# State products computed batch by batch in the layer's own layout, without a DRAM buffer, and the state tokens' weights split from resident tiles

## The chip, the cores and the metric

The kernel runs on one core of a Trainium2 chip. The metric is device time in microseconds (us), the lower the better. A core has five engines that run side by side and wait for each other through semaphores: PE (matrix products), ACT (ScalarE), DVE (VectorE), POOL (GpSimd) and SP, which here issues nearly all DMAs. PE reads its operands from SBUF (on-chip memory of 128 partitions) and writes into eight PSUM banks, from which ACT and DVE move results back to SBUF.

## The reference

Eight batches of cross attention between 512 tokens `x` and 32 state tokens, eight heads of 64, then two gated layers over all 544 tokens of a batch:

```python
a     = softmax(x @ state.T / 8);  xread = a @ state      # 512 rows a batch
a2    = softmax(state @ x.T / 8);  sread = a2 @ x         # 32 rows a batch
t     = concatenate([xread, sread])                       # heads side by side: 512 columns
h     = ((t @ w1) * (t @ w2)) @ w3 @ w_out                # first layer, d_ff 1024
out   = ((h @ w_a) * (h @ w_b)) @ moe2_w_out              # second layer, d_ff 1536
```

`x` and `state` are float32; the weights come as float64, two 32-bit words a number, and are turned into float32 on the chip. The products keep float32 accuracy: a number is split into a high and a low fp32r part (`split`), and three passes (high by high, high by low, low by high) replace one product.

## The kernel before

`w3 @ w_out` is multiplied out once (the weight products `wp`, kept as `ws`). For the x tokens, `xread @ w1` is never formed from `xread`: since `xread = a @ state`, the kernel computes the **state products** `P = state @ [w1 | w2]` per head and then multiplies by the attention weights `a`. A chunk (batch b, quarter q) of P holds, in 128 partitions (4 head pairs p of 32 state rows), two head rows r of 256 columns of w1 and 256 of w2. The layer uses it for two column blocks f (f // 2 is q).

How the state products come about. `state_product(p, nh, bg, i)` (L308) multiplies the transposed states of four batches (bg 0 or 1: 64 rows by 128 columns of `st_s`, the tile stT) with 512 columns of the converted tile `wk{p}_{nh}`: one call is two matmuls, r = 0 and 1, in the two halves of the array's rows, into two banks; as plain fp32 each is issued as two instructions. There are 4 p, 2 nh, 2 bg, 2 i: 32 calls. The result has four batches of one head pair below each other, while the layer wants one batch with its four pairs. So `product_move` (L323) copies a bank to a tile `sg` on ACT or DVE, `product_store` (L331) writes it to DRAM `p_d` in four pieces on SP's queue, `load_p` (L587) reads a chunk back, and `split_p` (L593) makes the high part on ACT and the low part on POOL.

Stages. First comes a **job stage**: jobs with guessed times are put in order by a planner (`run_jobs`, L643), which fixes each engine's order of instructions. The names in `EARLY` are loaded in that order: `wo` (rows of w_out), `w3`, `wk` (w1 and w2 by row block p and half nh) and the first three batches of x. ACT, DVE and POOL convert each; a `w3` block is then transposed by PE, split, and multiplied in a weight product of 24 matmuls. The stage also holds the attention of batches 0 and 1, the state products, and the whole first layer of batch 0 (`f`, then `x2f`). The products of bg 1 are its last filling, after the `f` jobs. Loads keep nine of the 47 SBUF units (4 KB a partition, `NUNITS`) free.

Then comes the **layer stage**: for b = 1 to 7 and f = 0 to 7, `step` (L1065) issues the product `ap` (6 matmuls), its copy on ACT, the filling `middle`, the product `bp` (6 matmuls), the product of both on DVE, the split of `h` (high on ACT, low on DVE), the filling `behind`, and at last `flush`, which accumulates the h of the step before into `x2p` (12 matmuls, four banks held for a batch). The fillings are written out by hand: the attention of the next batch in `MIDDLE` and `BEHIND`, `split_p` and `load_p` in `behind` at even f, and an `Intake` called `ab`, which converts the weights of the second layer when planned loads of the engines allow, 9 to 10 units being free. The state tokens' own rows (`one_s`, 256 columns) are interleaved with b = 7; their weights come from a second `Intake`, `sw`, which loads w1 and w2 once more by columns, converts and splits them. The second layer follows, with PE as its only busy engine.

Of the kernel before, what the change touches and what calls it, by code (L numbers as in the profile page):

```python
# [24 lines left out]
    "wo1 wo3 wo0 w3_1 wo2 w3_2 w3_0 wk0_0 x0 wk1_0 wk2_0 w3_3 "  # L25
    "w3_5 w3_6 x1 wk1_1 w3_4 wk3_0 wk0_1 x2 w3_7 wk3_1 wk2_1"
# [5 lines left out]
KEEP_SG = 2  # L32
KEEP_UNTIL = 40
STORE_BEHIND = 18

LATE_KEEP = 6
LATE_PRIO = 10
# [9 lines left out]
SW_TASKS = 2  # L47
SW_FROM = 46
# [5 lines left out]
P_AHEAD = 3  # L54
# [5 lines left out]
def attention_moe_moe2(  # L60
# [17 lines left out]
    nc = tc.nc  # L78
# [122 lines left out]
    p_d = [dp.tile([2, NP, NS, 2 * DFF1], F32, name=f"p_d{b}") for b in range(B)]  # L201
# [104 lines left out]
    sg = {}  # L306

    def state_product(p, nh, bg, i):  # L308

        for r in range(2):  # L310
            if i == 0:
                sg[p, nh, bg, r] = unit(f"sg{p}_{nh}_{bg}_{r}")
            t = pb[p, nh, bg, i, r] = bank(f"pb{p}_{nh}_{bg}_{i}_{r}")
            rows = slice(r * D, (r + 1) * D)
            nc.tensor.matmul(  # L315
                t,
                lhsT=st_s[rows, (bg * NP + p) * P : (bg * NP + p + 1) * P],
                rhs=conv[f"wk{p}_{nh}"].out[rows, half[i]],
                start=True,
                stop=True,  # L320
            )

    def product_move(p, nh, bg, i, r, eng):  # L323
        dst = sg[p, nh, bg, r].rearrange("p (q w c) -> p q w c", q=2, w=2)[:, :, i, :]
        src = flat(pb.pop((p, nh, bg, i, r)), 256)
        if eng == "A":
            nc.scalar.copy(dst, src)
        else:
            nc.vector.tensor_copy(dst, src)

    def product_store(p, nh, bg, r):  # L331
        for j in range(4):
            nc.sync.dma_start(
                out=p_d[4 * bg + j][r, p, :, nh * 1024 : (nh + 1) * 1024],
                in_=sg[p, nh, bg, r][j * NS : (j + 1) * NS],
            )
# [247 lines left out]
    p_raw = {}  # L584
    p_s = {}

    def load_p(b, q):  # L587
        t = unit(f"pr{b}_{q}")
        src = p_d[b].rearrange("r p n e -> (p n) r e")
        nc.sync.dma_start(out=flat(t, 512), in_=src[:, :, q * 512 : (q + 1) * 512])  # L590
        p_raw[b, q] = t

    def split_p(b, q):  # L593
        hi, lo = unit(f"ph{b}_{q}", F32R), unit(f"pl{b}_{q}", F32R)
        split(hi, lo, p_raw.pop((b, q)), nc.gpsimd)
        free(f"pr{b}_{q}", at=charge(A=1.1, G=2.4))
        p_s[b, q] = [t.rearrange("p (g w c) -> p g w c", g=2, w=2) for t in (hi, lo)]


# [123 lines left out]
    stores = {0: [], 1: []}  # L723

    def early_wk(p, nh):
        adds = convert_jobs(f"wk{p}_{nh}")
        last = []
        for bg in range(1):
            moves = {0: [], 1: []}
            for i in range(2):  # L730
                pr = Job(
                    "P",
                    1.0,
                    lambda a=(p, nh, bg, i): state_product(*a),
                    after=[adds[i], state_moved[bg]] + last[-1:],
                    need=2 - 2 * i,
                    keep=KEEP_SG,
                    prio=2 + len(loads) / 100,
                    banks=("ps", 2),
                )  # L740
                last.append(pr)
                for r in range(2):
                    moves[r].append(
                        Job(
                            "AV",
                            (0.6, 0.85),
                            lambda e, a=(p, nh, bg, i, r): product_move(*a, e),
                            after=[pr],
                            prio=0,
                        ).gives("ps", 1)  # L750
                    )
            for r in range(2):
                st = Job(
                    "D",
                    1.5,
                    lambda a=(p, nh, bg, r): product_store(*a),
                    after=moves[r],
                    prio=len(loads) + STORE_BEHIND,
                    lag=2.0,
                ).frees(f"sg{p}_{nh}_{bg}_{r}")  # L760
                if bg == 0:
                    stores[nh].append(st)
        return last

# [44 lines left out]

    wo_done = []  # L810
    products = []
    w_done = []
    for name in EARLY:
        if name[:2] == "wk":
            p, nh = int(name[2]), int(name[4])
            early_wk(p, nh)
# [226 lines left out]
    sw = Intake("sw", (w1, w2), None, list(range(NF1)))  # L1043
# [269 lines left out]
    last = None  # L1313
    for b, qs in ((0, range(4)), (1, range(3))):
        for q in qs:
            l = Job(
                "D",
                1.5,
                lambda b=b, q=q: load_p(b, q),
                after=stores[q // 2] + ([last] if last else []),  # L1320
                need=1,
                prio=1 + 20 * b,
                lag=1.0,
            )
            if b == 0 or q == 0:
                sp = Job("A", 1.1, lambda b=b, q=q: split_p(b, q), after=[l], need=2, prio=0 + 5 * b)
                ready[b, q] = last = Job("G", 2.4, nothing, after=[sp], prio=0 + 5 * b)
    lows = []
    mults = []
    for f in range(NF1):  # L1330
        pa = Job(
            "P",
            1.4,
            lambda f=f: first_product(f, 0),
            after=[ready[0, f // 2], attended[0][0]],
            banks=("ps", 1),
        )
# [9 lines left out]
    last = attended[0][0]  # L1347
    for p in range(NP):
        for nh in range(2):
            products = []  # L1350
            moves = {0: [], 1: []}
            for i in range(2):
                last = Job(
                    "P",
                    1.0,
                    lambda a=(p, nh, 1, i): state_product(*a),
                    after=[last],
                    need=2 - 2 * i,
                    keep=LATE_KEEP,
                    prio=LATE_PRIO,  # L1360
                    banks=("ps", 2),
                )
                products.append(last)
                for r in range(2):
                    moves[r].append(
                        Job(
                            "A", 0.6, lambda a=(p, nh, 1, i, r): product_move(*a, "A"), after=[last], prio=4
                        ).gives("ps", 1)
                    )
            frees_after(products, f"wk{p}_{nh}")  # L1370
            for r in range(2):
                Job(
                    "D",
                    1.7,
                    lambda a=(p, nh, 1, r): product_store(*a),
                    after=moves[r],
                    prio=len(loads) + STORE_BEHIND,
                    lag=2.0,
                ).frees(f"sg{p}_{nh}_1_{r}")
# [19 lines left out]
    chunks = [(b, q) for b in range(B) for q in range(4)]  # L1399

    for b in range(B):
# [9 lines left out]
        def fills1(f, b=b):  # L1411
            def middle():
                attend(MIDDLE, b, f)
                sw.run(HORIZON[0])
                ab.run(HORIZON[0])

            def behind():
                if f % 2 == 0:
                    c = 4 * b + f // 2
                    if c + 1 < len(chunks):  # L1420
                        split_p(*chunks[c + 1])
                    if c + P_AHEAD < len(chunks):
                        load_p(*chunks[c + P_AHEAD])
                        charge(D=1.5)
                else:
                    free(f"ph{b}_{f // 2}", f"pl{b}_{f // 2}")
                attend(BEHIND, b, f)
                if f == X_SLOT and b + 2 < B:
# [4 lines left out]
                if b == B - 2 and f == NF1 - 1:  # L1433
                    free("stT")
# [3 lines left out]
                if NF1 * b + f >= SW_FROM:  # L1438
                    sw.start(SW_TASKS, reserve=1)
                if NF1 * b + f >= AB_AT.get(ab.order[min(ab.next, NF2 - 1)], NF1 * B):  # L1440
                    ab.start(2, reserve=AB_RESERVE)
                sw.run(HORIZON[0])
# [13 lines left out]
    def pairs_s(f, i):  # L1456
        return [
            ([sw.cols[f][m][:, i, k, :] for m in range(2)], [sr_parts[q][:, k, :] for q in range(2)])
# [3 lines left out]
    def fills_s(f):  # L1462
        def middle():
            sw.run(HORIZON[1])
            ab.run(HORIZON[1])
            if f > 0:
                xf[0].run(1, keep=8 if sw.next < NF1 else 4)

        def behind():
            free(f"sw{f}h", f"sw{f}l")  # L1470
            sw.start(SW_TASKS, reserve=1)
            if sw.next == NF1 and f >= NF1 - 3:
# [310 lines left out]
```

## Time and profile before

| what | value |
|---|---|
| median of 3 runs | 1341.95 us (1341.14 to 1342.07) |
| profiled execution, its own time | 1342.51 us |
| its span, first to last instruction | 1340.7 us |
| PE busy in the span | 1300.3 us (97%) |
| DVE, ACT, POOL busy | 612.0, 550.2, 439.3 us |
| job stage (to the first `ap` of batch 1) | about 183 us |
| layer stage, batches 1 to 7 and the state tokens | about 183 to 560 us |
| second layer | about 560 to 1340.7 us |

The profile shows one execution. An engine's busy time is the union of its instructions; a matmul row of 0.39 us overlaps the next, which starts 0.22 to 0.23 us later. What "idle before" names is the event that ended the wait of that instruction.

### The profile page before, as it was taken

What the parts mean: (1) busy time and instruction counts of PE and PEld (TensorE: products, weight loads), DVE (VectorE), ACT (ScalarE), POOL (GpSimd) and SP (SyncE); (2) the same over time, 40 slices, a digit from 0 to 9 for tenths busy, and PEclk for the clock granted to TensorE, in tenths of its full rate; (3) what the DMA queues carried; (4) which work ended last, traced back from release to release, by engine and by line L of the source; (5) the groups of instructions that cost most, each with busy time, mean ns of one, the idle gap of its engine ahead of it and who ended that gap; (6) DMA issues with size and microseconds to landing.
All of it is one profiled execution on the core that took longest, in us unless ns stands there. A gap on an engine that the chain in (4) does not pass through costs nothing.

```text
span 1340.7 us, 17395 instructions
## 1 busy us (share of the span) xinstructions
PE 1300.3 (97%) x6596; PEld 1054.2 (79%) x6596; DVE 612.0 (46%) x792; ACT 550.2 (41%) x951; POOL 439.3 (33%) x352
## 2 busy tenths in 40 slices
PE   3998999999999999999999999999999999999998
PEld 1765768778777789888888888888888888888876
DVE  6676215646666667455532712232722326323240
ACT  7676455655565666354421412211422114221130
POOL 5554214454464477255510430110411103211100
PEclk6999999999999999999999999999999999999999
DMA  9977368493566552777373265542664434744301
GB/s 312 285 234 236 110 205 246 140 290 126 205 205 219 173 174 74 241 269 264 126 267 110 95 215 193 173 149 72 222 218 158 150 115 149 246 173 157 110 0 64
DMA packets 120662, 240.24 MB, mean 179 GB/s; under 512 B 44673, under 2 KB 65153, under 8 KB 120577
## 3 DMA queue, kind: packets, MB, share of 16 engines
q1 hardware_dynamic: 116000, 222.86, 50.5%
q0 software_dynamic: 4576, 16.26, 3.1%
q8 instruction: 52, 0.85, 0.2%
q14 instruction: 34, 0.27, 0.1%
HBM read 173.54 MB, written 65.54 MB: 178 GB/s over the span
## 4 chain that ended last, share of the span: by engine, by line
PE 89%; DMA 4%; DVE 3%; ACT 2%; issue 1%; POOL 1%; SPq 1%; ACTq 0%; POOLq 0%; DVEq 0%
PE r L1497 20%; PE o L1509 19%; PE v L1497 10%; PE x2p L1110 9%; PE bp L1051 5%; PE q L1497 5%; PE ap L1051 5%; PE abs L1552 3%; PE wp L358 2%; PE pb L315 2%; PE x2f L1291 2%; PE f L1051 1%; PE os L1581 1%; PE xt L388 1%; PE bs L1051 1%
## 5 line engine op out<-in xcount | busy, mean ns | idle before, releaser
L1509 PE MATMUL o<-z,h 128*128 128x512 f32 x1152 | 276.6, 389 | 1.3 <-ACT h L136 1.3
L1509 PEld LDWEIGHTS o<-z,h 128*128 128x128 f32 x1152 | 216.1, 188 | 47.0 <-ACT h L136 1.7
L1672 POOL TENSOR_TENSOR hb<-e,e 128x512 f32<-128x512 f32 x48 | 62.9, 1311 | 453.5 <-DVE e L1522 453.4
L136 ACT CAST h<-e 128x512 fp32r<-128x512 f32 x48 | 29.8, 621 | 364.8 <-DVE e L1675 350.8
L1110 PE MATMUL x2p<-hp,ws 128*128 128x512 f32 x672 | 161.9, 390 | 0.0
L1110 PEld LDWEIGHTS x2p<-hp,ws 128*128 128x128 f32 x672 | 125.8, 188 | 26.2
L142 POOL TENSOR_TENSOR pl<-pr,ph 128x512 fp32r<-128x512 f32 x64 | 83.1, 1320 | 120.6 <-ACT ph L136 74.0
L1522 DVE TENSOR_TENSOR e<-e,q 128x512 f32<-128x512 f32 x48 | 33.0, 688 | 195.7 <-PE q L1497 195.7
L1075 DVE TENSOR_TENSOR hfp<-asbp,bp 128x512 f32<-128x512 f32 x56 | 38.3, 684 | 93.6 <-PE bp L1051 89.9
L142 DVE TENSOR_TENSOR hp<-hfp,hp 128x512 fp32r<-128x512 f32 x56 | 54.1, 965 | 40.0 <-ACT hp L136 38.7
L1522 DVE TENSOR_TENSOR e<-e,v 128x512 f32<-128x512 f32 x48 | 33.0, 688 | 85.4 <-PE v L1497 85.4
L1497 PE MATMUL r<-xT2h,w 128*128 128x512 f32 x192 | 67.1, 390 | 0.0
L1497 PE MATMUL r<-xB11h,w 128*128 128x512 f32 x192 | 66.9, 389 | 0.0
L1497 PE MATMUL v<-xT1h,w 128*128 128x512 f32 x192 | 66.9, 389 | 0.0
L1497 PE MATMUL q<-xB21h,w 128*128 128x512 f32 x192 | 66.9, 389 | 0.0
L1497 PE MATMUL r<-xT3h,w 128*128 128x512 f32 x192 | 66.9, 389 | 0.0
L1497 PE MATMUL v<-xB22h,w 128*128 128x512 f32 x192 | 66.9, 389 | 0.0
L1497 PE MATMUL r<-xT4h,w 128*128 128x512 f32 x192 | 66.9, 389 | 0.0
L136 ACT CAST hp<-hfp 128x512 fp32r<-128x512 f32 x56 | 34.7, 620 | 57.0 <-DVE hfp L1075 52.2
L1069 ACT COPY asbp<-ap 128x512 f32<-128x512 f32 x56 | 33.1, 591 | 56.3 <-PE ap L1051 56.2
L142 DVE TENSOR_TENSOR h<-e,h 128x512 fp32r<-128x512 f32 x48 | 35.5, 739 | 33.4 <-ACT h L136 33.4
L1051 PE MATMUL bp<-ah,ph 128*128 128x512 f32 x112 | 47.9, 428 | 1.4 <-DVE a L473 0.9
(476 smaller groups left out, 2815.4 us busy)
## 6 DMA issues: line engine op xcount, KB each, us to landing
w<-w_d SPq DMA_DIRECT2D x168, 512.0 KB, 5.1
w_d<-w SPq DMA_DIRECT2D x48, 512.0 KB, 2.9
p_d<-sg SPq DMA_DIRECT2D x128, 128.0 KB, 2.5
pr<-p_d SPq DMA_DIRECT2D x32, 512.0 KB, 5.2
x<-in_x_dram SPq DMA_DIRECT2D x64, 128.0 KB, 4.6
sw<-in_moe_w_dram SPq DMA_DIRECT2D x16, 512.0 KB, 5.2
xB<-x_d SPq DMA_DIRECT2D x16, 512.0 KB, 4.8
x_d<-x2sp POOLq DMA_DIRECT2D x14, 512.0 KB, 5.8
```

Of the source, the lines that this page charges most:

```text
L136: nc.scalar.copy(hi, src)
L142: (eng or nc.vector).tensor_tensor(out=lo[:, i], in0=src[:, i], in1=hi[:, i].bitcast(F32), op=ALU.subtract)
L315: nc.tensor.matmul(t, lhsT=st_s[rows, (bg * NP + p) * P : (bg * NP + p + 1) * P], rhs=conv[f"wk{p}_{nh}"].out[rows, half[i]], start=True, ...
L1051: nc.tensor.matmul(dst[:, :n], lhsT=l[m], rhs=r[q], start=i == 0 and j == 0, stop=i == k - 1 and j == 2,)
L1069: nc.scalar.copy(a_sb[:, :n], pa[:, :n])
L1075: nc.vector.tensor_tensor(out=hf[:, :n], in0=a_sb[:, :n], in1=pb[:, :n], op=ALU.mult)
L1110: nc.tensor.matmul(acc[j], lhsT=w_s[f][:, m, j * P : (j + 1) * P], rhs=h[:, q, :n], start=per == 1 and f == 0 and i == 0, stop=f == NF1 - ...
L1497: nc.tensor.matmul(t, lhsT=w[m], rhs=xf[g].parts[x][q][:, k, :], start=first and k == 0 and i == 0, stop=k == 1 and i == 2, skip_group_che ...
L1509: nc.tensor.matmul(t, lhsT=h[:, m, part * P : (part + 1) * P], rhs=z_t[f][:, q, :], start=first and c == 0, stop=last and c == 2,)
L1522: nc.vector.tensor_tensor(out=out, in0=x, in1=y, op=ALU.add)
L1552: nc.tensor.matmul(t[:, w * 256 : (w + 1) * 256], lhsT=l[m], rhs=x_s[k][q], start=k == 0 and i == 0, stop=k == 3 and i == 2,)
L1672: nc.gpsimd.tensor_tensor(out=h2[-1][:, f % 2, :], in0=e2, in1=e5, op=ALU.mult)
```

## The change

`p_d`, `sg`, `product_move`, `product_store`, `load_p`, `split_p` and the intake `sw` go. A call `state_product(b, q)` now makes one chunk: 4 pairs p by 2 rows r, eight matmuls of 64 rows by 32 columns of `st_s` with 512 columns (two runs of 256) of `wk{p}_{q // 2}`; pair p goes to partitions 32p and up, r to the one or the other of two banks. `product_high` takes the high part from a bank on ACT, `product_low` the low part on DVE, straight from PSUM. There are again 32 calls: five in the job stage (batch 0 and the first chunk of batch 1), 27 in the layer stage, in `behind`, after the attention's filling and ahead of the `flush`, by the table `STEPS_P` (f = 0, 2, 3 and 4 of a batch; 0, 2, 3, 4, 5 in batch 6; 0 and 1 in batch 7). The eight `wk` tiles and stT stay in SBUF until batch 7. There `split_weights(nh)` splits four of them at f = 0 and four at f = 2, the low parts in turn on DVE and POOL, and the state tokens' step reads these. `EARLY` has a new order.

```diff
 EARLY = (
-    "wo1 wo3 wo0 w3_1 wo2 w3_2 w3_0 wk0_0 x0 wk1_0 wk2_0 w3_3 "
-    "w3_5 w3_6 x1 wk1_1 w3_4 wk3_0 wk0_1 x2 w3_7 wk3_1 wk2_1"
+    "wo0 wo1 wo2 w3_0 wo3 w3_1 x0 w3_2 wk0_0 w3_3 wk1_0 w3_4 wk2_0 "
+    "w3_5 wk3_0 w3_6 wk0_1 w3_7 wk1_1 x1 wk2_1 wk3_1 x2"
 ).split()
...
+STEPS_P = {0: [1], 2: [2], 3: [3], 4: [4]}
+STEPS_P_LAST = ({**STEPS_P, 5: [5]}, {0: [2], 1: [3]})
...
+    def state_product(b, q):
+
+        c = b // 4 * 512 + b % 4 * NS
         for r in range(2):
...
+            pb[b, q, r] = bank(f"pb{b}_{q}_{r}")
+        for p in range(NP):
+            for r in range(2):
+                rows = slice(r * D, (r + 1) * D)
+                w = conv[f"wk{p}_{q // 2}"].out[rows].rearrange("p (w q c) -> p w q c", w=2, q=2)
+                nc.tensor.matmul(
+                    flat(pb[b, q, r], 256)[NS * p : NS * (p + 1)],
+                    lhsT=st_s[rows, c + p * P : c + p * P + NS],
+                    rhs=w[:, :, q % 2, :],
+                    start=True,
+                    stop=True,
+                )
...
+    def product_high(b, q, r):
+        if r == 0:
+            parts = unit(f"ph{b}_{q}", F32R), unit(f"pl{b}_{q}", F32R)
+            p_s[b, q] = [t.rearrange("p (g w c) -> p g w c", g=2, w=2) for t in parts]
+        nc.scalar.copy(p_s[b, q][0][:, r], flat(pb[b, q, r], 256))
+
+    def product_low(b, q, r):
+        hi, lo = (t[:, r] for t in p_s[b, q])
+        nc.vector.tensor_tensor(
+            out=lo, in0=flat(pb.pop((b, q, r)), 256), in1=hi.bitcast(F32), op=ALU.subtract
+        )
...
+    def split_weights(nh):
+        for k in range(4):
+            hi, lo = unit(f"wkh{k}_{nh}", F32R), unit(f"wkl{k}_{nh}", F32R)
+            split(hi, lo, conv[f"wk{k}_{nh}"].out, ENGINES["VG"[k % 2]])
...
             def behind():
-                if f % 2 == 0:
-                    c = 4 * b + f // 2
-                    if c + 1 < len(chunks):
-                        split_p(*chunks[c + 1])
-                    if c + P_AHEAD < len(chunks):
-                        load_p(*chunks[c + P_AHEAD])
-                        charge(D=1.5)
-                else:
+                if f % 2:
                     free(f"ph{b}_{f // 2}", f"pl{b}_{f // 2}")
                 attend(BEHIND, b, f)
+                for q in slots.get(f, []):
+                    if 4 * b + q < 4 * B:
+                        now[0] += 1.2
+                        state_product(*divmod(4 * b + q, 4))
+                        until[0] = charge(A=1.2, V=1.4)
+                        for r in range(2):
+                            product_high(*divmod(4 * b + q, 4), r)
+                            product_low(*divmod(4 * b + q, 4), r)
+                        until[0] = None
+                if b == B - 1 and f in (0, 2):
+                    split_weights(f // 2)
```

## Rows read from the trace of the kernel before

**Rows 1.** The page's head and its first part: busy us (share) xinstructions, TensorE rows.

```profile
span 1340.7 us, 17395 instructions
PE 1300.3 (97%) x6596; PEld 1054.2 (79%) x6596; DVE 612.0 (46%) x792; ACT 550.2 (41%) x951; POOL 439.3 (33%) x352
```

**Rows 2.** By stage: window, length, busy PE, PEld, DVE, ACT, POOL, clock, DMA share, GB/s.

```profile
33.00:183.00 150.00, 143.43 (x723) 99.17 (x721) 76.24 (x101) 94.09 (x178) 56.19 (x44) 0.98 0.68 209
183.00:433.00 250.00, 246.50 (x1480) 196.23 (x1479) 151.82 (x190) 142.90 (x252) 121.23 (x100) 1.00 0.66 210
433.00:540.00 107.00, 106.82 (x681) 89.67 (x680) 68.07 (x78) 69.54 (x115) 71.02 (x52) 1.00 0.43 145
540.00:760.00 220.00, 219.77 (x1157) 189.54 (x1156) 99.13 (x146) 83.88 (x145) 75.06 (x62) 1.00 0.57 204
```

**Rows 3.** Waits of PE, 40 to 185 us: total us, times, longest.

```profile
PE w3t L344 <- POOL w L182: 2.4, 2, 2.0
PE f L1051 <- ACT ph L136: 2.3, 2, 1.8
PE f L1051 <- POOL pl L142: 1.6, 3, 0.7
```

**Rows 4.** The same windows view as rows 2, for 120 to 140 us.

```profile
120.00:140.00 20.00, 17.55 (x75) 13.87 (x74) 13.07 (x16) 12.70 (x24) 10.18 (x8) 0.91 0.42 136
```

**Rows 5.** Waits of PE, 185 to 560 us.

```profile
PE xt L388 <- issue: 1.4, 1, 1.4
PE bp L1051 <- DVE a L473: 0.9, 1, 0.9
```

**Rows 6.** PE in order of time: start, us, instruction; state products alone and in a row.

```profile
140.22 0.39 PE L1051 MATMUL f<-ah,pl 128*128 128x512 f32 x1
140.54 1.13 PE L315 MATMUL pb<-wk,stT 64*128 64x512 f32 x4
...
141.94 0.39 PE L1051 MATMUL f<-al,ph 128*128 128x512 f32 x1
...
173.35 9.71 PE L315 MATMUL pb<-wk,stT 64*128 64x512 f32 x44
182.99 0.50 PE L1051 MATMUL ap<-ah,ph 128*128 128x512 f32 x1
```

**Rows 7.** The chain that ended last, in order of time: one weight product.

```profile
60.98 5.68 PE wp L358 x24
```

**Rows 8.** Groups by line: xcount, busy us, mean ns of one, idle before and its releasers.

```profile
L315 PE MATMUL pb<-wk,stT 64*128 64x512 f32 x128 | 33.7, 615 | 0.3 <-ACT sg L327 0.3
L327 ACT COPY sg<-pb 128x512 f32<-128x512 f32 x53 | 27.8, 646 | 3.5 <-PE pb L315 3.5
L136 ACT CAST ph<-pr 128x1024 fp32r<-128x1024 f32 x32 | 33.5, 1048 | 5.0 <-DMA pr<-p_d 5.0
L142 POOL TENSOR_TENSOR pl<-pr,ph 128x512 fp32r<-128x512 f32 x64 | 83.1, 1320 | 120.6 <-ACT ph L136 74.0 <-DMA p_d<-sg 17.1 <-issue 14.5
L142 DVE TENSOR_TENSOR hp<-hfp,hp 128x512 fp32r<-128x512 f32 x56 | 54.1, 965 | 40.0 <-ACT hp L136 38.7 <-DMA x<-in_x_dram 1.4
L300 DVE TENSOR_TENSOR w3l<-w3t,w3h 128x512 fp32r<-128x512 f32 x16 | 10.8, 683 | 3.8 <-ACT w3h L294 3.7
L420 DVE TENSOR_REDUCE mx<-s 128x2 f32<-128x1024 f32 x8 | 9.7, 1210 | 0.0
```

**Rows 9.** PE in order of time: one call of `scores` between two products of the layer; the next batch's call.

```profile
186.98 0.39 PE L1051 MATMUL ap<-ah,pl 128*128 128x512 f32 x1
187.30 1.09 PE L404 MATMUL st<-xt,stT 64*32 64x512 f32 x16
...
188.66 0.39 PE L1051 MATMUL bp<-al,ph 128*128 128x512 f32 x1
...
236.66 1.09 PE L404 MATMUL st<-xt,stT 64*32 64x512 f32 x16
```

**Rows 10.** PE in order of time: the first call of `scores`.

```profile
55.48 2.36 PE L404 MATMUL st<-xt,stT 64*32 64x512 f32 x16
```

More of the change, by code (lines that the diff above doesn't have):

```diff
@@ L305, in attention_moe_moe2 @@
     pb = {}
-    sg = {}
-    def state_product(p, nh, bg, i):
+    def state_product(b, q):
+        c = b // 4 * 512 + b % 4 * NS
         for r in range(2):
[L311 to L327, printed above, removed]
-        else:
[L329 to L336, printed above, removed]
+            pb[b, q, r] = bank(f"pb{b}_{q}_{r}")
[10 more added lines that the diff above has]
+                )
+    p_s = {}
+    def product_high(b, q, r):
[8 more added lines that the diff above has]
+        )
     w3_b = {}
@@ L581, in attend @@
                 until[0] = None
[L584 to L597, printed above, removed]
     class Job:
@@ L721, in split_jobs @@
         return lows
[L723 to L763, printed above, removed]
     def frees_after(after, *names):
@@ L1312, in attention_moe_moe2 @@
     ready = {}
-    last = None
-    for b, qs in ((0, range(4)), (1, range(3))):
+    for b, qs in ((0, range(4)), (1, range(1))):
         for q in qs:
[L1316 to L1321, printed above, removed]
+            pr = Job(
+                "P",
+                1.2,
+                lambda b=b, q=q: state_product(b, q),
+                after=[*wk_done[q // 2], *state_moved.values()],
                 prio=1 + 20 * b,
-                lag=1.0,
+                banks=("ps", 2),
             )
-            if b == 0 or q == 0:
-                sp = Job("A", 1.1, lambda b=b, q=q: split_p(b, q), after=[l], need=2, prio=0 + 5 * b)
-                ready[b, q] = last = Job("G", 2.4, nothing, after=[sp], prio=0 + 5 * b)
+            ready[b, q] = []
+            for r in range(2):
+                h = Job(
+                    "A",
+                    0.65,
+                    lambda b=b, q=q, r=r: product_high(b, q, r),
+                    after=[pr] + ready[b, q],
+                    need=2 - 2 * r,
+                    prio=5 * b,
+                )
+                ready[b, q].append(
+                    Job("V", 0.75, lambda b=b, q=q, r=r: product_low(b, q, r), after=[h], prio=5 * b).gives("ps", 1)
+                )
     lows = []
@@ L1344, in attention_moe_moe2 @@
         lows.append(lo)
[L1347 to L1379, printed above, removed]
     moves = []
@@ L1463, in middle @@
         def middle():
-            sw.run(HORIZON[1])
             ab.run(HORIZON[1])
             if f > 0:
-                xf[0].run(1, keep=8 if sw.next < NF1 else 4)
+                xf[0].run(1, keep=4)
         def behind():
-            free(f"sw{f}h", f"sw{f}l")
-            sw.start(SW_TASKS, reserve=1)
-            if sw.next == NF1 and f >= NF1 - 3:
+            if f % 4 == 3:
+                free(*(f"wk{q}{k}_{f // 4}" for k in range(4) for q in "hl"))
+            if f >= NF1 - 3:
                 ab.start(1, reserve=5)
-            sw.run(HORIZON[1])
             ab.run(HORIZON[1])
-            xf[0].run(1, keep=8 if sw.next < NF1 else 4)
+            xf[0].run(1, keep=4)
             if f >= NF1 - 3 and (0, 0) not in w_t and room(5):
```

37 lines of the change are left out of this document (15 added, 22 removed).

## The prediction

> **What bounds the kernel.** The page's first part comes first: PE is busy for 1300.3 of 1340.7 us [rows 1]. Whatever the change takes from ACT, DVE, POOL and the DMA queues is worth only what it takes from PE's own work or from PE's 40 us of idle time, so the next views tell where these lie. By stage [rows 2], PE idles 6.6 us of the 150 from 33 to 183 us (150 - 143.43), 3.5 of the 250 up to 433, and 0.2 in each of the next two windows, where the state tokens and the second layer begin. The rest of the 40 lies before 33 us and at the end of the second layer. The changed order of loads still has three `wo`, a `w3`, the last `wo` and a `w3` in front, so I keep the start as it is; the end is not touched. The waits of PE say what the 6.6 us are: 2.4 for POOL's conversion of a `w3` block, 3.9 for the high and low parts of a chunk of the state products, at the `f` products [rows 3]. These 3.9 are the round trip through DRAM and POOL. In the same stretch the granted clock averages 0.91 for 20 us [rows 4]; around 129 us matmuls follow each other at half speed after those waits. I put the loss at no more than 20 x 0.09 = 1.8 us, 1.2 after leaving out the part in which PE was idle anyway. In the layer stage the waits are single events of 0.9 and 1.4 us [rows 5].
>
> **PE's own work.** The matmuls of the layer, of the weight products and of the state tokens stay as they are, in number and shape. Only the 32 calls of the state product change, and the trace has both shapes. The old one alone: the second `f` after it starts 1.72 us after the last `f` before it [rows 6]; two steps of 0.23 (5.68 less 0.39, by 23 [rows 7]) belong to the products themselves, which leaves 1.26 us. In a row, 44 instructions or 11 calls take 182.99 - 173.35 = 9.64 us, 0.88 a call [rows 6]. So a group costs 0.88 a call and 0.38 for going over to it and back. The 32 calls stand in 14 groups in order of time: 28.2 + 5.3 = 33.5 us, close to the 33.7 us of the line [rows 8]. The new shape, 64 rows by 32 columns, sixteen instructions, is that of `scores`: 188.66 - 186.98 - 0.46 = 1.22 us, alone between products of the layer [rows 9]. So the eight small tiles run side by side as well as the two wide ones. But 27 of the new calls stand alone, between `bp` and `x2p`: 27 x 1.22 = 32.9 us; the five in the job stage, in three groups, cost 5 x 0.88 + 3 x 0.38 = 5.5. That is 38.4 against 33.5: **+4.9 us**. Bounds: 0 if going over were free, +6.8 if all 32 cost the old single price of 1.26.
>
> On the 0.38 us, the Trainium skill (TensorEngine Tiling (Array Packing), Key Properties) says that a change of the tiling mode drains the array, and gives no price. That rule speaks against this change, which makes some 30 groups of 14; if the drain were free the forecast would be 5 us lower.
>
> **The job stage.** Eleven of its sixteen early calls, and all sixteen late ones, leave it; that work is in the sum above. What matters is its idle time. The 3.9 us of waits for chunks go: a chunk now needs its product (about 1), a cast on ACT (0.65, as the copy to `sg`) and a subtraction on DVE (0.68, as `w3l`, which also reads PSUM) [rows 8], against copy, store, load, a cast of 1.05 and two POOL passes of 1.32. With them goes the dip of the clock, 1.2. The 2.4 us at POOL's conversions can go, because 64 POOL passes leave, or grow, because PE has less to do in between. A `w3` block feeds PE for about 5.5 us of weight product [rows 7] and one of transposes; the new order brings one `w3` in every two names, and the eleven calls that used to fill such holes (eleven at 0.88 to 1.26, 10 to 14 us) are gone or moved. Bounds of the idle time left: 0 and 6.6 + 6.5 (half of these calls uncovered). ACT is busy 94 of the 150 us [rows 2] and loses some of its copies, so I stay near the lower end and leave 2.5 us. Gain: 6.6 + 1.2 - 2.5 = **-5.3 us**.
>
> **The layer stage.** Each call adds two casts on ACT and two subtractions on DVE, 64 x 0.65 = 42 and 64 x 0.68 = 44 us in all. ACT gives back more (27.8 + 33.5 us [rows 8]), POOL gives back 83.1 and gets only eight passes for the state tokens, SP loses 128 stores and 32 loads and with them every wait on them. DVE is the engine that pays: 151.8 busy of 250 us [rows 2] is 61%; with eight passes, 5.5 us, more in a batch of 236.66 - 187.30 = 49.4 us [rows 9] it comes to some two thirds of the then 54 us. That hides the sum, not each instruction: in `behind` at f = 2 and 3 the subtractions queue behind reductions and transposes of 1.21 us each [rows 8], with the next step's product of `ap` and `bp` behind them, and until they are done two PSUM banks are held beside the four of `x2p`, the one of `read` and the two of `ap` and `bp`. PE comes to the next `bp` about 2.7 (flush) + 1.4 (`ap`) + 1 us after the call, and the chain high, low, behind a transpose takes about 5: just covered. Bounds: -3.5 (even the present waits go, since POOL is quieter) and +9.8 (one wait like the 1.4 us of [rows 5] in each of seven batches). I take **+1 us**, nearer to a stage that now waits 3.5 us in 250.
>
> **State tokens.** `sw` goes: 16 loads of half a MB, conversion and splits, all hidden today (0.2 us idle in 433 to 540 [rows 2]), so nothing is gained. `split_weights` puts four casts of 1.05 us in a row on ACT, twice, ahead of the copy of the next `ap`; PE has a flush and two products (5.4 us) before it needs that copy's bank again. **+0.5 us**, between 0 and 2 x 1.5. The resident tiles cost units: at f = 1 I count 32 of 47 held, at f = 6 some 35, so `ab` often waits for its predecessor. I cost that at nothing: six blocks have seven batches of time, and a late one costs only if the second layer, idle 0.2 us in 220, has to wait.
>
> **Sum.** +4.9 - 5.3 + 1 + 0.5 = +1.1 on the span of 1340.7: 1341.8, with 1.8 us around it 1343.6. The profiled execution was 0.56 us above the median of the runs, so against the median the forecast is **1343.0 us**. A measurement of this kernel can tell about 0.2%, 2.7 us, from no change: within 1339.3 to 1344.6 it is "the same".
>
> **The rivals.**
> *Cover everywhere (faster).* All 7.8 us of the job stage and the 3.5 of the layer stage go: 1341.95 + 4.9 - 7.8 - 3.5 = 1335.6. For it: the DVE pass on `hp` averages 0.965 us where its neighbour `w3l` of the same size takes 0.683 [rows 8], so something slows DVE that may be the 64 POOL passes. The Trainium skill (SBUF — State Buffer, Who interferes with whom) says that a DVE instruction with two SBUF inputs and a GpSimd instruction reading SBUF lock each other out; by it `hp` is slowed by POOL, and `product_low`, with one input in PSUM, is not. Against it: 27 more DVE pairs in the queue. Chance 0.31.
> *Starved job stage (slower).* The fillers are missing before the chunks are ready: the 7.8 us are not gained and half of the moved calls leave holes, 6.5. 1341.95 + 4.9 + 6.5 + 1.5 = 1355; it decides once a `w3` block takes longer to be loaded and converted than the 6.5 us that PE lives on it. Partly so, 1347. Chance 0.18.
> *DVE and banks in the layer stage (slower).* A third of a microsecond at each of 27 calls: +9 in place of the +1, 1351. For it: the queue at f = 2 and 3; against it: DVE's load. Chance 0.13.
> *The tiles don't run side by side.* The first `scores` took 2.36 us [rows 10]. At that price 32 calls cost 32 x 1.14 more, 1379. That call probably waited for the second half of its operand; the one in the layer took 1.09. Chance 0.03.
> About even has 0.35. So faster 0.31, same 0.35, slower 0.34. The range takes in the full gain and most of the slower cases: 1334 to 1354; the likeliest case alone is 1339 to 1345.
>
> **What would show it.** PE's waits for `ph` and `pl` at the `f` products are gone, the clock in that stage is 1.0, and the first `ap` comes at about 183 - (33.5 - 5.5) - 5.3, some 150 us. A group of sixteen instructions of the new product between `bp` and `x2p` costs 1.2 us, and a batch 49.4 + 4 x 1.22 = 54.3 us. No waits of `bp`, `ap` or `x2p` on DVE's low parts; PE's idle time in the layer stage under 6 us. Wrong would be: `w3t` or `wp` waiting for conversions for more than 5 us in all, `bp` or the product waiting for banks, or an `ab` block that comes late in the second layer.

## The result

The changed kernel takes **1357.99 us** (median of 4 runs, 1357.88 to 1358.09) against 1342.01 us of the kernel before in the same session: a ratio of 1.0117, 95% interval 1.0100 to 1.0135. It is slower by 16 us, outside the forecast range of 1334 to 1354.

The page of the changed kernel, against [rows 1]:

```profile
span 1356.0 us, 17687 instructions
PE 1310.8 (97%) x6980; PEld 1050.2 (77%) x6980; DVE 617.4 (46%) x829; ACT 507.0 (37%) x898; POOL 336.0 (25%) x272
```

POOL gave back 103 us and ACT 43 us, and the time became longer: as the prediction has it at its start, what the other engines give back is worth only what PE gains by it. PE is busy 10.5 us longer and idle 4.8 us longer.

The stages are best cut at three instructions of PE: the first weight product `wp`, the first `ap` of batch 1, the first `r` of the second layer. In the kernel before these stand at 32.70, 182.99 and 561.10 us. After, the windows view (columns as in [rows 2]) cut at the same three:

```profile
0.00:28.90 28.90, 9.31 (x35) 5.38 (x35) 16.96 (x22) 21.50 (x38) 16.23 (x17) 0.65 1.01 288
28.90:152.84 123.94, 114.68 (x675) 90.46 (x674) 79.88 (x106) 74.00 (x141) 48.20 (x35) 0.96 0.47 158
152.84:567.29 414.45, 411.48 (x2735) 308.97 (x2733) 235.86 (x319) 199.18 (x370) 101.78 (x85) 1.00 0.30 102
567.29:760.00 192.71, 184.74 (x940) 157.50 (x939) 75.52 (x119) 68.58 (x118) 66.94 (x54) 0.98 0.59 211
760.00:1356.00 596.00, 590.61 (x2603) 487.89 (x2601) 209.16 (x267) 143.73 (x233) 102.81 (x83) 1.00 0.43 147
```

| stretch | before | after | difference | forecast |
|---|---|---|---|---|
| to the first `ap` | 182.99 | 152.84 | -30.15 | -33.3 |
| layer and state tokens | 378.11 | 414.45 | +36.34 | +34.4 |
| second layer | 779.60 | 788.71 | **+9.1** | 0 |
| span | 1340.7 | 1356.0 | +15.3 | +1.1 |

The forecasts are the prediction's terms by stretch: -28.0 and -5.3; 27 x 1.22, +1 and +0.5; nothing. The sum is 14.2 us off: 9.1 in a stage in which the change edits nothing, 3.2 ahead of the first `ap`, 1.9 in the layer stage.

PE's waits of after, from the first `wp` to the first `ap`, then from 567 us to the end (total, times, longest):

```profile
PE w3t L338 <- POOL w L177: 6.0, 4, 2.3
PE wp L352 <- DVE w3l L294: 2.9, 1, 2.9
...
PE r L1416 <- ACT e L1556: 6.0, 1, 6.0
PE r L1416 <- DVE e L1441: 1.7, 1, 1.7
PE o L1428 <- ACT h L131: 1.3, 1, 1.3
```

The `f` products wait for the state chunks no more, so the DRAM round trip of [rows 3] is gone as forecast; conversions of `w3` wait in its place. In the second layer the last line stood before too; the two `r` lines are new. What PE waits for at 687 us, in order of time on all engines:

```profile
681.00 1.41 POOL L894 TENSOR_TENSOR ab8s<-ab 128x256 f32<-128x256 f32 x2
...
684.97 1.04 ACT L131 CAST w<-ab8s 128x1024 fp32r<-128x1024 f32 x1 [2.85 <-POOL ab8s L894]
...
686.22 0.62 ACT L131 CAST z<-ab8t 128x512 fp32r<-128x512 f32 x1 [0.20 <-POOL ab8t L177]
686.74 0.58 ACT L1556 COPY e<-r 128x512 f32<-128x512 f32 x1
687.37 0.80 PE L1416 MATMUL r<-xT2h,w 128*128 128x512 f32 x1 [5.96 <-ACT e L1556]
```

ACT was not busy: it stood at `ab8`'s cast for 2.85 us until POOL had made the sums, and the copy `e` that frees PE's bank was queued behind. It is the conversion of the last block of the second layer's weights (an `ab` block), made inside the second layer. After the wait PE runs at about half rate for a while (matmul starts 0.4 to 0.6 us apart up to 690 us, in place of 0.22 to 0.23); the granted clock of the 20 us around it is 0.83:

```profile
680.00:700.00 20.00, 14.04 (x59) 11.48 (x59) 7.21 (x9) 4.62 (x8) 7.40 (x7) 0.83 0.70 249
```

Over the whole second layer PE is idle 6.3 us longer than in the kernel before and, with the same 3542 matmuls, busy 2.8 us longer; together these are the 9.1 us.

### The profile page after: what moved, and what is told of

Same layout as the page of the kernel before. It is cut to its first block, busy times and chain, and to the rows that moved or that the text cites. A ratio compares the mean times of both kernels' runs of the same rounds, so it can differ in the third digit from the quotient of the medians.

```text
span 1356.0 us, 17687 instructions
## 1 busy us (share of the span) xinstructions
PE 1310.8 (97%) x6980; PEld 1050.2 (77%) x6980; DVE 617.4 (46%) x829; ACT 507.0 (37%) x898; POOL 336.0 (25%) x272
## 4 chain that ended last, share of the span: by engine, by line
PE 88%; ACT 5%; DVE 4%; issue 1%; POOL 1%; DMA 1%; SPq 0%; POOLq 0%; DVEq 0%; ACTq 0%
PE o L1428 19%; PE r L1416 19%; PE x2p L1045 10%; PE v L1416 9%; PE bp L986 5%; PE ap L986 5%; PE q L1416 5%; PE pb L310 2%; PE wp L352 2%; PE abs L1471 2%; PE x2f L1226 2%; PE f L986 2%; PE os L1500 1%; PE bs L986 1%; PE as L986 1%
## 5 line engine op out<-in xcount | busy, mean ns | idle before, releaser
L1045 PE MATMUL x2p<-hp,ws 128*128 128x512 f32 x672 | 165.7, 395 | 0.0
L137 DVE TENSOR_TENSOR hp<-hfp,hp 128x512 fp32r<-128x512 f32 x56 | 44.5, 795 | 40.1 <-ACT hp L131 40.1
L177 POOL TENSOR_TENSOR ab<-ab,ab 128x512 int32<-128x512 int32 x24 | 31.5, 1332 | 74.0 <-ACT asbp L1004 33.3
L137 POOL TENSOR_TENSOR al<-a,ah 128x512 fp32r<-128x512 f32 x16 | 22.8, 1444 | 107.1 <-ACT ah L131 102.2
```

The source lines that it names most:

```text
L137: (eng or nc.vector).tensor_tensor(out=lo[:, i], in0=src[:, i], in1=hi[:, i].bitcast(F32), op=ALU.subtract)
L177: nc.gpsimd.tensor_tensor(out=out, in0=out, in1=d.bitcast(I32), op=ALU.add)
L1045: nc.tensor.matmul(acc[j], lhsT=w_s[f][:, m, j * P : (j + 1) * P], rhs=h[:, q, :n], start=per == 1 and f == 0 and i == 0, stop=f == NF1 - ...
```

## The experiments

### Why the second layer lost 9 us

*The old intake of the state tokens' weights* (e1_sw). The resident `wk` tiles are no longer split and are given back in batches 6 and 7; `sw` loads, converts and splits w1 and w2 by columns as before, and the conversion of the second layer's tokens keeps eight units off, as before, until `sw` is through. The main lines:

```diff
-                if b == B - 1 and f in (0, 2):
-                    split_weights(f // 2)
...
+                if NF1 * b + f >= 46:
+                    sw.start(2, reserve=1)
```

> The changed kernel with the old intake of the state tokens' weights: sixteen loads and splits of `sw` in the shape of before from step 46 on, no resident split tiles, and the raw wk tiles given back at batch 6 and at the first steps of batch 7. The products, their places and the job stage stay as changed. Theory 1 (the 9.1 us that the second layer gained come from units: the resident tiles hold what the intake of `ab` needs, and its late blocks are forced while PE waits): the second layer goes back to some 780 us, its waits of 6.0 and 1.7 us go, and the time is 1348 to 1350 us; the layer stage stays as it is after the change. Rival (the late blocks are late for another reason, such as the conversions themselves being slower or the early blocks starting late): second layer 786 to 790 us, 1356 to 1359 us.

Measured: 1347.52 us, ratio to before 1.0051 (1.0034 to 1.0067). The second layer begins at 567.47 and takes 778.1 us, and both `r` waits are gone. The issue of the first two late `ab` blocks on SP's queue shows the difference: in the kernel before, in the changed kernel, and here.

```profile
530.39 0.37 SPq L890 DMA_DIRECT2D ab<-in_moe_w_b_dram  x1
554.12 0.38 SPq L890 DMA_DIRECT2D ab<-in_moe_w_b_dram  x1
```

```profile
556.11 0.38 SPq L826 DMA_DIRECT2D ab<-in_moe_w_b_dram  x1
565.20 0.38 SPq L826 DMA_DIRECT2D ab<-in_moe_w_b_dram  x1
...
656.25 0.39 SPq L826 DMA_DIRECT2D ab<-in_moe_w_b_dram  x1
```

```profile
534.01 0.37 SPq L826 DMA_DIRECT2D ab<-in_moe_w_b_dram  x1
560.49 0.38 SPq L826 DMA_DIRECT2D ab<-in_moe_w_b_dram  x1
```

Before, the first late load leaves 31 us ahead of the second layer, after the change 11 us, here 33 us. (The last row of the second fence is the last of the six late blocks, for later.) So putting `sw` back cures it. Two things came back with it, its smaller holding of units and the eight units that the tokens' conversion keeps off; e9_reserve4 below leaves both as the change has them. That sixteen loads with their conversions and splits came back cost little: layer and state tokens 415.5 in place of 414.45.

*Asking earlier and for less* (e2_abstart):

```diff
-            if f >= NF1 - 3:
-                ab.start(1, reserve=5)
+            if f >= NF1 - 5:
+                ab.start(1, reserve=1)
```

The conversion of the second layer's tokens (`xf[0].run`) keeps ten units off in place of four.

> The changed kernel with resident tiles, but in the state tokens the late `ab` blocks are started from step 11 on with one unit in reserve instead of from step 13 with five, and the conversion of the second layer's tokens keeps ten units off. Theory 1 in the form that units are only handed out late in this stage: the late blocks start 10 to 20 us earlier, the second layer loses 3 us or less, 1351 to 1354 us. Rival (units are really short until all split tiles are given back at step 15): no block starts more than 5 us earlier, 1356 to 1360 us.

Measured: 1362.85 us, ratio 1.0162 (1.0146 to 1.0177). The first late load leaves at 512.2 us, 44 us earlier, and the second layer is worse, 794.7 us:

```profile
PE abs L1471 <- ACT xs L131: 5.8, 1, 5.8
PE o L1428 <- DMA z<-z_d: 5.4, 1, 5.4
```

Both sides of the expectation missed: a block did start early, and the loss grew. The waits are now for the state tokens' operand `xs` and for a load of `z`. That the units given to `ab` are missing elsewhere, in the tokens' conversion first of all, is the likely reason, but the run changed three numbers at once and doesn't show it.

*One unit* (e9_reserve4). `ab.start` asks for 6 vacant units and the reserve. By the planner's own list, behind step 5 of the state tokens the kernel before holds 35 of 47 units (six of them `sw` tiles), and gives back two of the six just ahead of the ask: 14 are vacant where 11 are asked for. (The twelve of the expectation below is the count ahead of that.) The changed kernel holds 37 there, eight of them split `wk` tiles, which it gives back only behind step 7: 10 are vacant behind steps 5 and 6, and the start slips to step 7.

```diff
-                ab.start(1, reserve=5)
+                ab.start(1, reserve=4)
```

> The changed kernel with one number changed: the late ab blocks may start when 6 + 4 units are vacant in place of 6 + 5. Counted from the planner's own list, ten units are vacant behind steps 5 and 6 of the state tokens with the change, twelve behind step 5 before it; eleven are asked for. Theory (the second layer's loss is this one unit): the first late block's load goes out some 25 us earlier than at 556, near 530 to 535, and the second layer gains back 5 to 9 us, 1348 to 1353 us. Rival (the units are short for the whole stage, so that an earlier block only takes them from the conversion of the second layer's tokens, as in e2_abstart): the second layer stays at 786 us or more, 1356 to 1363 us.

Measured: 1346.98 us, ratio 1.0033 (1.0019 to 1.0047).

```profile
529.75 0.38 SPq L826 DMA_DIRECT2D ab<-in_moe_w_b_dram  x1
564.64 0.38 SPq L826 DMA_DIRECT2D ab<-in_moe_w_b_dram  x1
...
651.92 0.39 SPq L826 DMA_DIRECT2D ab<-in_moe_w_b_dram  x1
```

The first late block leaves at 529.75, the second layer takes 1344.5 - 566.32 = 778.2 us, and the `r` waits are gone. The second late block leaves when it did, but the last one, whose conversion PE waited for, leaves 4.3 us earlier (651.92 for 656.25). Nothing else was changed: one unit in a request decided over 10.5 us.

### What the order of loads does

*The old order in the changed kernel* (e3_early): `EARLY` is that of the kernel before.

```diff
-    "wo0 wo1 wo2 w3_0 wo3 w3_1 x0 w3_2 wk0_0 w3_3 wk1_0 w3_4 wk2_0 "
...
+    "wo1 wo3 wo0 w3_1 wo2 w3_2 w3_0 wk0_0 x0 wk1_0 wk2_0 w3_3 "
...
```

> The changed kernel with the order of loads of the kernel before, and nothing else. If the 3.8 us that the start gained come from the new order (the first token block seventh instead of ninth), the first weight product is at 32.7 us again. If the waits for conversions of `w3` (9.3 us) come from the new order, they fall below 4 us; if they come from the missing products that used to fill such holes, they stay between 6 and 12 us. The first: about 1357, the first `ap` at 150 to 152 us; the second: 1361 to 1364, the first `ap` at 156 to 158 us.

Measured: 1355.84 us, ratio 1.0108 (1.0093 to 1.0123). The first `wp` stands at 32.64 again, PE waits 4.5 us for `w3` in place of 9, and the first `ap` comes at 151.46:

```profile
32.64:151.46 118.82, 114.09 (x675) 89.65 (x674) 74.67 (x100) 70.23 (x134) 43.13 (x33) 0.97 0.47 148
```

The first `ap` is where the first theory had it and the time 1.2 us below its value, but the waits fall only about half way, between the values of the two: the late start and the shorter waits cancel. With the old order PE makes four groups of `w3` transposes before its first product, with the new one two, and does the others later. The other kernels here that share the job stage of the changed one have their first `ap` at 151.26 to 152.84, so the two orders are equal, and the forecast (149.7) is missed by 1.6 to 3.2 us, depending on the run.

*All `w3` in a row* (e7_w3first), on top of e1_sw:

```diff
+    "wo0 wo1 wo2 w3_0 wo3 w3_1 w3_2 w3_3 x0 w3_4 w3_5 w3_6 w3_7 "
+    "wk0_0 wk1_0 wk2_0 wk3_0 x1 wk0_1 wk1_1 wk2_1 wk3_1 x2"
```

> On top of e1_sw only the order of loads: all eight w3 blocks ahead of the wk tiles, the first token block ninth. The first ap came at 151.3 to 152.8 us with the changed order and at 151.5 with the order of before, so these two are equal to it. Theory: PE's 5 to 9 us of waits for conversions of w3 come from wk tiles loaded and converted between the w3 blocks, whose products no longer fill such holes; w3 in a row takes these waits below 2 us and the first ap comes at 146 to 149 us, 1342.5 to 1345.5 us. Rival: the wk tiles then come too late and PE waits for them before the first state product or for the tokens' attention; the first ap at 151 to 156 us, 1347 to 1352 us.

Measured: 1342.37 us, ratio 1.0000 (0.9990 to 1.0009). The first `ap` comes at 147.17; PE idles 1.75 us in this stage, all of it for `wk` conversions before a state product (two waits, 1.8 us):

```profile
32.83:147.17 114.34, 112.59 (x675) 87.94 (x674) 68.94 (x100) 70.20 (x134) 42.30 (x33) 0.98 0.48 154
```

*The same order in the kernel before* (e12_before_w3), the edit above and no other:

> The kernel before with the order of loads of e7_w3first and nothing else. Theory: that order is only good without the round trip through DRAM; here the state products come some 40 us later, their chunks are stored and read back after the other work of the stage is used up, and PE waits for them at the first f products: first ap at 188 to 205 us in place of 183, 1347 to 1362 us. Rival (the order alone is what gained, and the kernel before would gain the same 5 us): first ap at 177 to 179, 1336 to 1338 us.

Measured: 1343.34 us, ratio 1.0004 (0.9994 to 1.0014); first `ap` at 185.79, 2.8 us later than with its own order. PE has one wait of 11 us there; with it, SP's and ACT's rows of that time:

```profile
PE srt L517 <- ACT sn L510: 11.0, 1, 11.0
...
99.65 13.54 SPq L333 DMA_DIRECT2D p_d<-sg  x27
113.30 0.38 SPq L590 DMA_DIRECT2D pr<-p_d  x1
...
118.75 1.05 ACT L136 CAST ph<-pr 128x1024 fp32r<-128x1024 f32 x1 [10.27 <-issue]
...
120.36 0.48 PE L517 MATMUL srt<-ident,sn 128*128 128x128 f32 x1 [11.03 <-ACT sn L510]
```

The first chunk is loaded behind 27 stores on SP's queue; ACT stands at its cast for 10.27 us, with the `sn` that PE needs queued behind. (The profile names no event that ended ACT's wait. That it was this load is read from the order of the rows.) From the first `wp` to the first `ap` PE is idle 12.8 us in place of 6.6 and busy 3.6 us less. So the order alone gains nothing there, and the waits fall on the DRAM round trip; the loss is smaller than the range that was expected. The same order gained 5.2 us with the changed products, so with the change an order of loads pays that gained the kernel before nothing. It was just not given that order.

### What a product costs in the layer stage

*Each state product twice* (e4_double), into the same two banks:

```diff
+    single = state_product
...
+    def state_product(b, q):
+        single(b, q)
+        for p in range(NP):
...
```

> Every state product's sixteen matmuls are issued twice in a row into the same two banks, which takes nothing from any other engine and adds no new change of shape. If a lone call is 0.88 us of matmuls and some 0.4 us for going over and back, the profile's group of a call grows by about 0.9 us and the layer step by the same: 27 x 0.9 + 5 x 0.9 = 28 to 29 us, 1386 us. If the cost lies in each matmul, a call doubles its 1.25 us: 40 us, 1398 us. The second layer stays at about 789 us in both.

Measured: 1384.37 us (one run), first `ap` 4.1 us later and layer stage 22.1 us longer than after. One doubled call:

```profile
229.76 1.09 PE L310 MATMUL pb<-wk,stT 64*32 64x512 f32 x16
230.65 1.06 PE L327 MATMUL pb<-wk,stT 64*32 64x512 f32 x16
231.64 3.01 PE L1062 MATMUL x2p<-hp,ws 128*128 128x512 f32 x12
```

The second sixteen cost 0.89 us here, and a step with a doubled call, where nothing else waits, is 0.84 longer (steps 0, 2 and 3: 7.54, 8.35, 8.34 in place of 6.70, 7.51, 7.50). A lone call costs 1.26: the step behind which it was put grew by that, 5.44 to 6.70, 6.25 to 7.50. So 0.85 is the product and 0.41 is going over and back, as the prediction had it from [rows 6] (0.88 and 0.38). In all the kernel is 26.4 us longer than after, a little under the 28 expected.

*Where the queues of DVE and ACT make it dearer.* In the changed kernel step 4 of a batch takes 7.6 to 8.4 us in batches 2 to 5, 6.92 in batch 6. Step 3's queue of DVE in batch 2, then ACT's and PE's rows of step 4:

```profile
233.65 1.21 DVE L437 TENSOR_REDUCE m<-t 128x32 f32<-128x1024 f32 x1
234.90 1.22 DVE L438 TENSOR_TENSOR t<-t,m 128x1024 f32<-128x1024 f32 x1
...
236.12 1.27 DVE L328 TENSOR_TENSOR pl<-pb,ph 128x512 fp32r<-128x512 f32 x2
...
233.51 1.07 ACT L324 CAST ph<-pb 128x512 fp32r<-128x512 f32 x2
234.61 0.58 ACT L1004 COPY asbp<-ap 128x512 f32<-128x512 f32 x1
...
235.25 0.50 PE L986 MATMUL bp<-ah,ph 128*128 128x512 f32 x1 [0.57 <-ACT asbp L1004]
236.84 1.68 PE L310 MATMUL pb<-wk,stT 64*32 64x512 f32 x16
```

The low parts of the product behind step 3 (236.12) stand behind a reduction and a subtraction of 1.2 us each; until they are done its banks are held, and step 4's product takes 1.68 in place of 1.09. Step 4's `bp` comes late too, but by the profile it waits 0.57 us for ACT's copy of `ap`, which stands behind the two casts of the same state product: three such waits of `bp` make 1.7 us of the layer stage, and one for `pl` 0.5. So both halves of `product_high` and `product_low` cost time by their place in a queue. That the product's own 0.59 us are a wait for banks is read from the kernel; the profile shows no releaser for it.

*Other places* (e5_places), on top of e1_sw, steps 0, 2, 4 and 6:

```diff
-STEPS_P = {0: [1], 2: [2], 3: [3], 4: [4]}
...
+STEPS_P = {0: [1], 2: [2], 4: [3], 6: [4]}
...
```

> On top of e1_sw only the places of the state products in a batch: behind steps 0, 2, 4 and 6 instead of 0, 2, 3 and 4 (batch 6 also behind 7). Theory: the 0.4 to 1.5 us that step 4 loses in every batch are PE waiting for PSUM banks and for ACT, because the product behind step 3 is followed by one behind step 4 while DVE still has the row maxima, the sums and the low parts in its queue. Then step 4 falls to 6.9 us (5.6 + 1.3), step 3 to 6.25, step 6 rises to 7.6, and the layer stage gains 4 to 6 us: 1341.5 to 1343.5 us. Rival: the wait belongs to the read's transpose at step 4 and ACT, and stays there or moves to step 6: within 1 us of 1347.5.

Measured: 1359.12 us, ratio 1.0121 (1.0096 to 1.0147), 12 us worse. Step 4 does fall, to 6.8 to 7.5, and step 3 to 6.24, but step 6 takes 10.8 to 12.3 us in place of 6.33 (batches 2 to 5):

```profile
247.80 1.03 PE L382 MATMUL xt<-ident,x 128*128 128x128 f32 x8
250.13 1.04 PE L310 MATMUL pb<-wk,stT 64*32 64x512 f32 x2
252.54 0.68 DVE L1011 TENSOR_TENSOR hfp<-asbp,bp 128x512 f32<-128x512 f32 x1
253.28 1.09 PE L310 MATMUL pb<-wk,stT 64*32 64x512 f32 x14 [2.10 <-DVE hfp L1011]
254.51 0.68 DVE L388 COPY xt<-xt 128x512 f32<-128x512 f32 x1
```

The transposes of the tokens at 247.80 hold two banks that are copied out behind the step; with them, four of `x2p` and one of `bp`, the product finds one bank, and its other fourteen matmuls wait until DVE has read `bp`. The wait for `hfp`, DVE's reading of `bp`, is in the rows; the count of banks is read from the kernel. Neither theory had counted the banks that are free at the new place.

*Both* (e8_both), these places and the `w3` order, on top of e1_sw:

> e1_sw with the places of e5_places and the loads of e7_w3first. If the two are independent the gains add: 1336 to 1342 us, at or below the 1341.3 us of the kernel before. If neither holds, 1347 to 1352 us.

Measured: 1352.11 us, ratio 1.0080 (1.0050 to 1.0110). It was a third outcome: one gains, the other loses. The order of loads gains 7.0 here and gained 5.2 alone; the places cost 9.7 here and cost 11.6 alone.

*The product ahead of the maxima behind step 3* (e10_front), on top of e7_w3first:

```diff
-                attend(BEHIND, b, f)
+                if f != 3:
+                    attend(BEHIND, b, f)
                 for q in slots.get(f, []):
...
+                if f == 3:
+                    attend(BEHIND, b, f)
```

> On top of e7_w3first only this: behind step 3 the state product with its casts and low parts is issued ahead of the row maxima, their subtraction and the read's move, in place of behind them. Theory: step 4 waits because the low parts of the product behind step 3 stand in DVE's queue behind a reduction and a subtraction of 1.2 us each, so that PSUM banks come free late; then step 4 falls from 7.6 to 8.4 us to 6.9 to 7.0 in batches 2 to 6, and the time by 3.5 to 6 us, 1336.5 to 1339 us. Rival: the row maxima come late instead and ACT's exponential behind step 4's copy holds the next copy up; step 4 or 5 keeps the loss, 1341 to 1344 us.

Measured: 1344.72 us, ratio 1.0015 (1.0006 to 1.0024), where 1.0000 stood: no gain. Step 4 falls to 6.83 to 7.26 as expected, but step 5 rises from 6.35 to 7.04 to 7.13, and a new wait of 2.3 us stands in the state tokens (`bs` for DVE's `hfp`). Over batches 1 to 6 the steps are 2.35 us shorter than in e7_w3first, and batch 7 with the state tokens is 3.1 us longer. DVE's queue of steps 3 and 4 in batch 2:

```profile
227.13 1.28 DVE L328 TENSOR_TENSOR pl<-pb,ph 128x512 fp32r<-128x512 f32 x2
228.32 1.21 DVE L437 TENSOR_REDUCE m<-t 128x32 f32<-128x1024 f32 x1
...
233.04 1.21 DVE L450 TENSOR_REDUCE sum<-t 128x32 f32<-128x1024 f32 x1
235.12 1.29 DVE L328 TENSOR_TENSOR pl<-pb,ph 128x512 fp32r<-128x512 f32 x2
```

The first pair of `pl` leads now; the second still stands behind `sum` and the reciprocal that waits for ACT, and step 5's `a2t` waits for it. The rival was right that the loss moves on, though not in the way it said. Step 5 takes some 2.9 us of it in four batches, the state tokens take 3.1. In this kernel `sw` runs there; e11_all below, without `sw`, has no such wait, and what links the two was not tested.

### The parts together

*The changed kernel with `w3` in a row, the order behind step 3 and the reserve of 4* (e11_all), three edits that are shown above:

> The changed kernel (resident weight tiles, no intake for the state tokens) with the loads of e7_w3first, the order of e10_front behind step 3 and the reserve of e9_reserve4. If all three theories hold, 1336 to 1341 us, below the kernel before; if the units stay short, 1344 to 1350 us.

Measured: 1339.31 us, ratio 0.9974 (0.9964 to 0.9983): 0.26% faster than the kernel before, as expected if all three hold. First `ap` at 146.93, layer and state tokens 412.0, second layer 778.2.

*Ahead of the sums behind step 4 too* (e13_front34):

```diff
-                if f != 3:
+                if f not in (3, 4):
                     attend(BEHIND, b, f)
```

> e11_all with the product ahead of the attention's vector work behind step 4 as well as behind step 3. In e11_all step 5 rose from 6.35 to 7.05 us in batches 2 to 6, where the column transposes wait for low parts behind the sums' reduction. Theory (one queue, and only the order in it matters): step 5 falls back to 6.35 to 6.5 us, four to five batches by 0.6, 2.5 to 3 us in all: 1336 to 1337.5 us. Rival (DVE is full there, so that the wait moves on to step 6 or 7 through the row's normalisation): 1338.5 to 1341 us.

Measured: **1337.65 us**, ratio 0.9962 (0.9951 to 0.9974). Step 5 is back at 6.33 to 6.34; step 7 rises (it took 6.37 to 6.82 in batches 2 to 5 and takes 6.80 to 7.22), so about half is kept. The intervals of these two overlap, and that the second is the faster rests on the steps of the profile. Of its stages:

```profile
32.80:147.80 115.00, 113.19 (x676) 88.35 (x674) 68.94 (x100) 70.35 (x134) 42.26 (x33) 1.00 0.48 154
147.80:558.38 410.58, 409.09 (x2735) 308.38 (x2734) 234.80 (x320) 201.26 (x374) 103.19 (x86) 1.00 0.30 102
```

This kernel has the lowest time of the study. It is the change as it was made, with three edits that move no work from one engine to another.

## Why the prediction was wrong

**The failed step** is "The resident tiles cost units [...] I cost that at nothing: six blocks have seven batches of time, and a late one costs only if the second layer has to wait." The condition was the right one, and a late block was named as a sign of being wrong, but the units were counted at two steps of the layer, for the early blocks, and not at the steps of the state tokens, where the late blocks ask. At the ask behind step 5 the split tiles held four units more than `sw` did, and three were spare. The term measured +9.1 us in place of nothing. Shown by putting back `sw` (second layer 778.1) and by lowering the request by one (778.2). No rival named it either: all four lay in the stages that the change edits.

**PE's own work** was right in mechanism and nearly in size. A lone call costs 1.26 us, not 1.22, which makes 1.1 us over 27 calls. The five calls of the job stage stand in two groups, not three. PE's busy time up to the first `ap` fell by 29.4 us (9.68 + 143.72 to 9.31 + 114.68), forecast 28.0. That the tiles don't run side by side is refuted (the rows of sixteen take 1.09). A group of these tiles costs 0.41 us beyond its products, which the doubled call does not pay twice. The Trainium skill (TensorEngine Tiling (Array Packing), Key Properties) says that a change of the tiling mode drains the array. The doubled call agrees with it; that the 0.41 us are such a drain no run shows.

**The job stage.** The 3.9 us of waits for chunks went as forecast. "I stay near the lower end and leave 2.5 us" is the term that was mis-sized: 9.3 us of idle time from the first `wp` in place of 2.5, 4.7 with the old order, and the clock at 0.96, not 1.0. The bound of 13.1 held, and one sign of being wrong stood: `w3t` and `wp` wait 8.9 us for conversions. The reason given, one `w3` in two names and the fillers gone, is what `w3` in a row removed (1.75 us). "I keep the start as it is" was wrong by 3.8 us and cost nothing, because the transposes it left out came later.

**The layer stage.** Forecast +1, measured 36.3 - 34.0 = +2.3: over batches 1 to 6 the steps add up to 298.2 before and 332.0 after, +33.8, of which 25 calls are 31.5. The place was right, low parts behind reductions of 1.21 us, and "just covered" was too hopeful in four batches of six, by 0.8 to 1.5 us at step 4; some of that was ACT's queue, which the prediction had not priced in this stage. Against it, steps 5 to 7 of batch 5 are 3.2 us shorter than before. Of the state tokens' +0.5 nothing is seen: batch 7 and the tokens together grew by 82.48 - 79.94 = 2.54, the price of the two calls there.

**The rivals.** *Cover everywhere* did not come. Its sign did: the mean DVE pass on `hp`, 0.965 us in [rows 8], is 0.795 now, and `pl`, which reads PSUM, takes 0.677:

```profile
L137 DVE TENSOR_TENSOR hp<-hfp,hp 128x512 fp32r<-128x512 f32 x56 | 44.5, 795 | 40.1 <-ACT hp L131 40.1
L328 DVE TENSOR_TENSOR pl<-pb,ph 128x512 fp32r<-128x512 f32 x64 | 40.6, 677 | 1.9 <-ACT ph L324 1.1
```

That is 9.6 us of DVE (54.1 to 44.5), and no wait of PE in the layer stage of the kernel before was for these passes. The median pass takes 0.693 us in both kernels; it is the long passes that became shorter (the longest 2.594 us before, 1.716 after). The Trainium skill (SBUF — State Buffer, Who interferes with whom) says that a DVE instruction with two SBUF inputs contends with a GpSimd instruction that reads SBUF. The direction agrees with it; no run varied POOL alone, so the cause isn't shown. *Starved job stage* and *DVE and banks* both came in part, 3.2 and 1.3 us.

Without the 10.5 us of the one unit the change is worth +0.33% (1346.98 us), in place of the forecast +0.1%. In the profiled execution of that run the job stage is 2.2 us and the layer stage 1.9 us above the forecast, and the second layer 1.4 us below.

## What to carry to other kernels

When a change makes something resident, count what is vacant at every later point where somebody asks with a threshold, against what is asked for, also in stages the change does not touch: here 10 against 11 cost 10.5 us. The price of inserting work into a full step can lie in its free banks and its place in the queues of the engines that empty them, more than in its own duration: the same product cost 1.26 us behind one step and 4.5 to 6 behind another. When a dependency is removed, re-plan the order of loads that it had dictated, because the gain may lie in the order it now permits.

## What the runs showed of the chip

The granted clock of the first slice of the page was 0.6 to 0.7 in twelve of the fourteen profiles and 0.9 or more in two, those of the kernel before with `w3` first and of the last kernel. The first `wp` came no earlier for it (32.85 and 32.80 us, against 32.28 to 32.83 in the kernels with the same order at the lower clock): ahead of it PE waits 13.9 to 14.8 us for a conversion on POOL. The doubled calls show that a repeated group of the small tiles costs 0.84 to 0.89 us where the first costs 1.26.
